# Attention backward for two blocks: x^T and g^T from transposing DMAs, all transfers on one chained queue, group products 512 + 128 wide

## The chip, the cores and the metric

The kernel runs on one core of one Trainium2 chip. The metric is the device time of one execution, in microseconds (us). Each kernel was run several times, and before every comparison the kernel before was run on the same chip in the same rounds. Executions of one kernel differ by up to 15 us in the worst case, so differences of a few us in the whole are read with their intervals.

A ratio is the mean time of one kernel's runs over that of the kernel before in the same rounds. It is therefore not quite the ratio of the medians that are quoted beside it. The experiments ran in other rounds than the kernel after, on three chips, and the median of the kernel before went from 1711.5 to 1713.9 us between them; where a run is compared with after, the ratios are therefore the better measure.

## The reference

Two independent attention blocks, A and B, of the same shape; the outputs are laid side by side. The kernel returns the output and the gradients of all ten inputs for a given `grad_out`.

```python
B, Sq, D = 8, 96, 640            # x: [8, 96, 640]
H, Sk, Dh = 32, 512, 128         # k_cache, v_cache: [8, 32, 512, 128]
def _A_ref(x, k_cache, v_cache, wq, wo):          # _B_ref is the same
    q = (x @ wq).reshape(B, Sq, H, Dh).transpose(0, 2, 1, 3)
    scores = einsum("bhqd,bhkd->bhqk", q, k_cache) * Dh ** -0.5
    p = softmax(scores)
    o = einsum("bhqk,bhkd->bhqd", p, v_cache)
    return o.transpose(0, 2, 1, 3).reshape(B, Sq, H * Dh) @ wo
out = concatenate([_A_ref(...), _B_ref(...)], axis=-1)      # [8, 96, 1280]
# returned: out and d(x, k, v, wq, wo) of both blocks, for grad_out [8, 96, 1280]
```

All inputs and outputs are bf16.

## The kernel before

The kernel handles block A, then block B. In a block it works through 32 heads, in pairs that share loads and in groups of four that share the products with wo and wq (here "group products", which sum into `out` and `dx`). One head and one batch entry is a "tick": scores, softmax, and the four gradient products for 96 queries and 512 keys. There are 2 x 32 x 8 = 512 ticks. The instructions are placed by a table of ticks (`em.add(tick, slot, fn)`), so loads, transposes and products of different heads are interleaved in one static order for each engine.

The parts that the change and the argument touch:

```python
class Chain:                       # keeps the issue order of the sync queue as written
    def __call__(self, res):
        ins = getattr(res, "ins", res)
        if self.last is not None:
            self.tc.add_manual_dep(ins, self.last.name, ..., reason="issue order")
        self.last = ins
        return res
...
    def setup_ld(which_, c):       # block B: a column chunk of x or g, by GpSimd
        ...
            nc.gpsimd.dma_start(tmp[:], src_flat[:, c * 128:(c + 1) * 128].rearrange("(t p) d -> p t d", p=128))
    def setup_T(which_, c):        # x^T and g^T by TensorE, 6 transposes a chunk, and a copy on VectorE
        ...
            for t0 in range(0, TT, 8):
                ...
                    nc.tensor.transpose(pt[:, i * 128:(i + 1) * 128], tmp[:, t0 + i, :], ident[:])
                nc.vector.tensor_copy(dst[:, c, t0 * 128:(t0 + nt) * 128], pt[:, 0:nt * 128])
...
    def pA(h):                     # the weights of a head, by GpSimd
            nc.gpsimd.dma_start(wo_h, wo[h * 128:(h + 1) * 128, :])
            ...
                    nc.gpsimd.dma_start(wq_p[:], wq_v[:, :, h * 128:(h + HP) * 128])
...
    def p_st(h, b, which):         # stores of dV and dK of a pair, on the chained sync queue
            sp(nc.sync.dma_start(dst.rearrange("h (p c) d -> p h (c d)", c=KC), t_[:]))
...
                st["dK_p"] = wk.tile([128, HP, KC * 128], BF16, name="dK_sb", bufs=3)   # dV_sb: bufs=3 too
...
    gsplits = [(0, 256), (256, 256), (512, 128)]      # built by a loop in the kernel
    def gU(g, which, t, gi):       # group products, 256 + 256 + 128 wide
            ...
            else:                  # last group: each piece is stored by GpSimd at once
                ob = wk.tile([128, w], BF16, name="ob", bufs=4)
                nc.vector.tensor_tensor(ob[:], o_ps[:], acc[:, t, c0:c0 + w], op=ALU.add)
                nc.gpsimd.dma_start(dst_flat[t * 128:(t + 1) * 128, c0:c0 + w], ob[:])
```

The loads of K, V (natural and transposed) and the stores of dK and dV are on the sync queue already; the transposed forms KT and VT come from transposing DMAs.

Of the kernel before, what the change touches and what calls it, by code (L numbers as in the profile page):

```python
# [8 lines left out]
ALU = mybir.AluOpType  # L9
AX = mybir.AxisListType  # L10
F32 = mybir.dt.float32
BF16 = mybir.dt.bfloat16
# [3 lines left out]
class Emitter:  # L16
# [28 lines left out]
HP = 2  # L45
HK = [
    dict(pA=-10, pB=-7, pC0=[-6, -4], pC1=[-5, -3], pD1=-2, pD0=0, qA0=21, qA1=25, qB=[28, 25], qD=[(26, 0, 2), (27, 2, 5)]),
    dict(pA=-4, pB=-2, pC0=[-1, 3], pC1=[1, 2], pD1=3, pD0=6, qA0=29, qA1=33, qB=[36, 33], qD=[(34, 0, 2), (35, 2, 5)]),
# [23 lines left out]
def build_block(tc, em, tick0, blk, x, kc, vc, wq, wo, g_all, out_all, dx, dk, dv, dwq, dwo, ident, ones, pools, HG=4, first=True, groups=None):  # L72
# [47 lines left out]
    stp = pools["stp"]  # L120
    sp = pools["sp"]

    def setup_ld(which_, c):
        def f():
            src_flat = x_flat if which_ == 0 else g_flat
            tmp = stp.tile([128, TT, 128], BF16, name="ld_tmp")
            with nc.allow_non_contiguous_dma(reason="setup column chunk"):
                nc.gpsimd.dma_start(tmp[:], src_flat[:, c * 128:(c + 1) * 128].rearrange("(t p) d -> p t d", p=128))
            S[("tmp", which_, c)] = tmp
        return f  # L130

    def setup_T(which_, c):
        def f():
            key = "xT" if which_ == 0 else "gT"
            if c == 0:
                S[key] = const.tile([128, DC, T], BF16, name=key, bufs=1)
            dst = S[key]
            if first:
                tmp = S["x_nat" if which_ == 0 else "g_nat"][:, :, c * 128:(c + 1) * 128]
            else:  # L140
                tmp = S.pop(("tmp", which_, c))
            for t0 in range(0, TT, 8):
                nt = min(8, TT - t0)
                pt = bank([128, 8 * 128], BF16, "tp_ps")
                for i in range(nt):
                    nc.tensor.transpose(pt[:, i * 128:(i + 1) * 128], tmp[:, t0 + i, :], ident[:])
                nc.vector.tensor_copy(dst[:, c, t0 * 128:(t0 + nt) * 128], pt[:, 0:nt * 128])
        return f

    def setup_nat(which_):  # L150
        def f():
# [3 lines left out]
            (nc.sync if first else nc.gpsimd).dma_start(t_[:], src_flat.rearrange("(t p) d -> p t d", p=128))  # L155
# [8 lines left out]
    for c in range(DC):  # L164
        if not first:
            em.add(tick0 - 12 + c - 2, SL_LOAD, setup_ld(0, c))
            em.add(tick0 - 11 + c - 2, SL_LOAD, setup_ld(1, c))
        em.add(tick0 - 12 + c, SL_SETUP, setup_T(0, c))
        em.add(tick0 - 11 + c, SL_SETUP, setup_T(1, c))
    em.add(tick0 + (-15 if first else 21), SL_LOAD, setup_nat(1))  # L170
    em.add(tick0 + (-16 if first else 20), SL_LOAD, setup_nat(0))
# [10 lines left out]
    def pA(h):  # L182
        def f():
# [4 lines left out]
            nc.gpsimd.dma_start(wo_h, wo[h * 128:(h + 1) * 128, :])  # L188
            j = h % HP
            if j == 0:  # L190
                wq_p = hd.tile([128, DC, HP * 128], BF16, name="wq_p", bufs=2)
                with nc.allow_non_contiguous_dma(reason="per-pair wq slice"):
                    nc.gpsimd.dma_start(wq_p[:], wq_v[:, :, h * 128:(h + HP) * 128])
# [266 lines left out]
    def qB(h, di):  # L460
        def f():
            st = HS[(blk, h)]
            Onat = st["Onat"]
            if "dwo_sb" not in st:
                st["dwo_sb"] = hd.tile([128, D], BF16, name="dwo_sb")
                st["dwo_n"] = 0
# [6 lines left out]
            st["dwo_n"] += 1  # L473
            if st["dwo_n"] == len(dsplits):
                nc.gpsimd.dma_start(dwo[h * 128:(h + 1) * 128, :], dwo_sb[:])  # L475
        return f

    def qD(h, c_lo, c_hi):
        def f():
# [4 lines left out]
            if "dwq_sb" not in pr:  # L484
                pr["dwq_sb"] = hd.tile([128, DC, HP * 128], BF16, name="dwq_sb", bufs=1)
                pr["dwq_n"] = 0
# [9 lines left out]
            pr["dwq_n"] += ncn  # L496
            if pr["dwq_n"] == DC * HP:
                with nc.allow_non_contiguous_dma(reason="per-pair dwq slice"):
                    nc.gpsimd.dma_start(dwq_v[:, :, (h - j) * 128:(h - j + HP) * 128], dwq_sb[:])  # L499
# [8 lines left out]
    gsplits = []  # L508
    c0_ = 0
    while c0_ < D:  # L510
        w_ = 256 if D - c0_ >= 256 else 128
        gsplits.append((c0_, w_))
        c0_ += w_

    def gU(g, which, t, gi):
        def f():
            acc = S.get("out_acc" if which == 0 else "dx_acc")
            dst_flat = out_flat if which == 0 else dx_flat
            (c0, w) = gsplits[gi]
# [199 lines left out]
```

## Time and profile before

The kernel before takes 1711.03 us (three runs, 1708.27 to 1713.91); the profiled run spans 1706.8 us.

The page's first and third part (busy time and share of the span for each engine; the DMA queues with packets, MB and the time of their packets as a share of 16 engines' span):

```profile
PE 1633.9 (96%) x22648; PEld 1359.3 (80%) x22648; DVE 1388.8 (81%) x3597; ACT 1345.0 (79%) x3529; POOL 713.3 (42%) x1306
...
q1 hardware_dynamic: 304672, 404.75, 91.3%
q0 software_dynamic: 15648, 49.83, 8.2%
```

TensorE is busy 96% of the span, but the DMA queues' shares also sum to about 1. The view by windows (the stretch, its length, the busy time and instruction count of each engine, the granted TensorE clock, the DMA share and GB/s):

```profile
core 0: us, PE busy (x) PEld busy (x) DVE busy (x) ACT busy (x) POOL busy (x), PEclk, DMA share, GB/s
...
25.00:109.00 84.00, 76.61 (x1066) 61.38 (x1065) 69.66 (x175) 76.93 (x201) 35.14 (x65) 1.00 1.01 267
109.00:211.00 102.00, 101.03 (x1411) 84.03 (x1409) 79.11 (x193) 92.21 (x253) 41.48 (x76) 1.00 1.05 280
...
778.00:954.00 176.00, 158.38 (x2144) 131.19 (x2142) 134.14 (x345) 125.25 (x324) 89.57 (x158) 0.96 0.98 264
954.00:1055.00 101.00, 100.22 (x1399) 83.31 (x1397) 78.30 (x191) 91.38 (x252) 41.13 (x76) 1.00 1.03 278
...
1664.00:1707.00 43.00, 30.29 (x388) 25.80 (x385) 23.40 (x62) 9.09 (x24) 25.20 (x46) 0.90 0.29 106
```

In the stretch from 109 to 211 us TensorE is busy 101.03 of 102 us. In the first 84 us after the start it is busy 76.61 only. At the seam of the blocks (778 to 954) TensorE is idle 17.6 us and the clock falls to 0.96. At the end the DMAs move 106 GB/s and the clock falls to 0.90.

The waits at the seam (780 to 930 us; waiting engine, line and tile <- releaser: us in total, times, longest), and the longest of VectorE's as a row of its timeline (start, duration, engine, line, operation, count, [idle before <- releaser]):

```profile
DVE ob L536 <- DMA out_dram<-ob: 6.1, 4, 2.7
PE tp_ps L146 <- DMA ld_tmp<-in_B_x_dram: 5.8, 4, 3.0
```

```profile
908.77 0.43 DVE L536 TENSOR_TENSOR ob<-o_ps,dx_acc 128x256 bf16<-128x256 f32 x1 [2.71 <-DMA out_dram<-ob]
```

VectorE waits for the narrow output stores of block A, which stand behind the 960 KB loads of x_nat and g_nat on GpSimd's queue; TensorE waits for the chunks that it is to transpose.

### The profile page before, as it was taken

How to read it: one execution, taken by the hardware profiler on the slowest of the kernel's cores; microseconds unless marked ns; L12 is line 12 of the kernel's file. 1: busy time of each engine (PE TensorE's matmuls, PEld its weight loads, DVE VectorE, ACT ScalarE, POOL GpSimd, SP SyncE). 2: the span in 40 equal slices, each digit the busy share in tenths (PEclk: the TensorE clock that was granted, in tenths of full speed). 3: DMA queues.
4: the chain of work that ended last, by engine and by line, in shares of the span. 5: the costliest groups of instructions: out<-in, count | busy, mean ns of one | idle time of the engine just before them, and what ended most of it. 6: DMA issues, size and time to landing. Idle time of an engine off the chain costs nothing. (4 is left out here: it accounts for less than half of the span.)

```text
span 1706.8 us, 59407 instructions
## 1 busy us (share of the span) xinstructions
PE 1633.9 (96%) x22648; PEld 1359.3 (80%) x22648; DVE 1388.8 (81%) x3597; ACT 1345.0 (79%) x3529; POOL 713.3 (42%) x1306
## 2 busy tenths in 40 slices
PE   6999999999999999998998999999999999999997
PEld 4788888887888888786876888878888788887876
DVE  4887888888888888887876878888888888888885
ACT  4988977878788787875876989787787877878782
POOL 3443343444334443344464444343443343443345
PEclk9999999999999999999998999999999999999999
DMA  9999999999999999999999999999999999999992
GB/s 257 278 277 279 281 271 274 286 285 273 280 266 267 284 267 275 266 276 264 251 284 273 274 269 291 266 265 284 275 272 268 270 271 289 269 273 276 255 258 106
DMA packets 320608, 458.38 MB, mean 269 GB/s; under 512 B 37217, under 2 KB 300897, under 8 KB 312129
## 3 DMA queue, kind: packets, MB, share of 16 engines
q1 hardware_dynamic: 304672, 404.75, 91.3%
q0 software_dynamic: 15648, 49.83, 8.2%
q8 instruction: 177, 2.90, 0.7%
q14 instruction: 111, 0.90, 0.1%
HBM read 161.09 MB, written 159.12 MB: 188 GB/s over the span
## 5 line engine op out<-in xcount | busy, mean ns | idle before, releaser
L313 ACT ACTIVATE E_sb<-S_ps,negm 96x512 bf16<-96x512 f32 x512 | 349.7, 683 | 218.7 <-DVE negm L303 208.9
L332 POOL TENSOR_SCALAR P_sb<-E_sb,rinv 96x512 bf16<-96x512 bf16 x512 | 354.3, 692 | 318.8 <-DVE rinv L323 313.4
L386 POOL TENSOR_TENSOR prod<-OT_h,dOT_h 128x96 bf16<-128x96 bf16 x512 | 188.1, 367 | 532.6 <-DVE OT_h L358 527.9
L400 DVE SCALAR_TENSOR_TENSOR dS_sb<-dP_ps,dl_ps,P_sb 96x512 bf16<-96x512 f32 x512 | 382.2, 746 | 30.0 <-PE dl_ps L398 17.7
L303 DVE TENSOR_REDUCE negm<-S_ps 96x1 f32<-96x512 f32 x512 | 347.9, 680 | 43.8 <-PE S_ps L301 42.8
L443 ACT ACTIVATE dK_sb<-dK_ps 128x512 bf16<-128x512 f32 x512 | 302.6, 591 | 74.1 <-PE dK_ps L438 70.4
L377 ACT ACTIVATE dV_sb<-dV_ps 128x512 bf16<-128x512 f32 x512 | 308.1, 602 | 0.3 <-PE dV_ps L372 0.2
L361 ACT ACTIVATE PT_sb<-optp_ps 128x384 bf16<-128x384 bf16 x512 | 252.3, 493 | 0.7 <-PE optp_ps L355 0.5
L372 PE MATMUL dV_ps<-dOnat_h,P_sb 96*128 96x128 bf16 x2048 | 198.7, 219 | 0.0
L438 PE MATMUL dK_ps<-Qnat_h,dS_sb 96*128 96x128 bf16 x2048 | 198.4, 219 | 0.0
L422 PE MATMUL dq_dst_ps<-ident,dS_sb 96*128 96x96 bf16 x2048 | 172.8, 206 | 25.9 <-DVE dS_sb L400 23.9
L396 PE MATMUL dP_ps<-VT_p,dOT_h 128*96 128x512 bf16 x512 | 195.7, 382 | 0.0
L301 PE MATMUL S_ps<-KT_p,QT_h 128*96 128x512 bf16 x512 | 194.5, 380 | 0.4
L424 DVE COPY dST_sb<-dq_dst_ps 128x384 bf16<-128x384 bf16 x512 | 177.6, 347 | 12.9 <-PE dq_dst_ps L422 12.1
L355 PE MATMUL optp_ps<-ident,P_sb 96*128 96x96 bf16 x2048 | 172.2, 206 | 2.4 <-POOL P_sb L332 1.7
L348 PE MATMUL optp_ps<-PT_sb,V_sb 128*128 128x96 bf16 x2048 | 172.3, 206 | 0.9 <-ACT PT_sb L361 0.8
L415 PE MATMUL dq_dst_ps<-dST_sb,K_sb 128*128 128x96 bf16 x2048 | 170.9, 206 | 1.7 <-DVE dST_sb L424 1.5
L525 PE MATMUL o_ps<-wo_r,OT_h 128*128 128x256 bf16 (+1 forms) x1152 | 150.5, 254 | 1.4
L415 PEld LDWEIGHTS <-K_sb 128*128 128x128 bf16 x2048 | 134.1, 98 | 21.8 <-issue 2.6
L525 PE MATMUL o_ps<-wqT_h,dQT_h 128*128 128x256 bf16 (+1 forms) x1152 | 150.3, 255 | 0.5 <-DVE ob L536 0.5
L358 DVE CAST OT_h<-optp_ps 128x96 bf16<-128x96 f32 x512 | 126.7, 247 | 19.3 <-PE optp_ps L355 16.0
L422 PEld LDWEIGHTS <-dS_sb 96*128 96x128 bf16 x2048 | 114.8, 98 | 33.7 <-DVE dS_sb L400 32.2
(77 smaller groups left out, 3369.7 us busy)
## 6 DMA issues: line engine op xcount, KB each, us to landing
out_dram<-dV_sb SPq DMA_DIRECT2D x256, 256.0 KB, 4.5
out_dram<-dK_sb SPq DMA_DIRECT2D x256, 256.0 KB, 4.9
V_sb<-in_A_v_cache_dram SPq DMA_DIRECT2D x128, 256.0 KB, 4.8
K_sb<-in_A_k_cache_dram SPq DMA_DIRECT2D x128, 256.0 KB, 4.8
V_sb<-in_B_v_cache_dram SPq DMA_DIRECT2D x128, 256.0 KB, 4.8
K_sb<-in_B_k_cache_dram SPq DMA_DIRECT2D x128, 256.0 KB, 4.8
out_dram<-dwo_sb POOLq DMA_DIRECT2D x64, 160.0 KB, 4.9
out_dram<-dwq_sb POOLq DMA_DIRECT2D x32, 320.0 KB, 6.0
```

Of the source, the lines that this page charges most:

```text
L303: nc.vector.tensor_reduce(negm[:], S_ps[:], axis=AX.X, op=ALU.max, negate=True)
L313: nc.scalar.activation(E_sb[:].rearrange("q (a f) -> q a f", f=F4), st["S_ps"][:].rearrange("q (f a) -> q a f", f=F4), ACT.Exp, bias=st["n ...
L332: nc.gpsimd.tensor_scalar(P_sb[:], st["E_sb"][:], st["rinv"][:], 0.0, op0=ALU.mult, op1=ALU.add)
L361: nc.scalar.activation(PT_sb[:], PT_ps, ACT.Identity, scale=1.0)
L372: nc.tensor.matmul(dV_ps[:, c * 128:(c + 1) * 128], P_sb[:, c * 128:(c + 1) * 128], hs["dOnat_h"][:, b * 128:(b + 1) * 128], start=True, s ...
L377: nc.scalar.activation(dV_p[:, j], dV_ps[:], ACT.Identity, scale=1.0)
L400: nc.vector.scalar_tensor_tensor(dS_sb[:].rearrange("q (a f) -> q a f", f=F4), dP_ps[:].rearrange("q (f a) -> q a f", f=F4), dl_ps[:, 0:1] ...
L415: nc.tensor.matmul(dQT_ps, st["K_sb"][:, c, :], st["dST_sb"][:, c * Sq:(c + 1) * Sq], start=(c == 0), stop=(c == KC - 1))
L422: nc.tensor.transpose(dST_ps[:, c * Sq:(c + 1) * Sq], dS_sb[:, c * 128:(c + 1) * 128], ident[0:Sq, 0:Sq])
L438: nc.tensor.matmul(dK_ps[:, c * 128:(c + 1) * 128], dS_sb[:, c * 128:(c + 1) * 128], hs["Qnat_h"][:, b * 128:(b + 1) * 128], start=True, s ...
L443: nc.scalar.activation(dK_p[:, j], dK_ps[:], ACT.Identity, scale=1.0)
L525: nc.tensor.matmul(o_ps[:], src[:, t * 128:(t + 1) * 128], rhs, start=(hh == 0), stop=(hh == groups[g] - 1))
```

## The change

The intent is to take work off TensorE and VectorE (the transposes of x and g and their copies), to take all DMA issue off GpSimd, and to have fewer and wider group products with one store of 640 columns for three narrow ones. The core of the diff:

```diff
     def setup_T(which_, c):
-            dst = S[key]
-            ...                      # x_nat/g_nat (block A) or ld_tmp (block B), 6 transposes, copy
-                    nc.tensor.transpose(pt[:, i * 128:(i + 1) * 128], tmp[:, t0 + i, :], ident[:])
-                nc.vector.tensor_copy(dst[:, c, t0 * 128:(t0 + nt) * 128], pt[:, 0:nt * 128])
+            src_flat = x_flat if which_ == 0 else g_flat
+            sp(nc.sync.dma_start_transpose(S[key][:, c, :], src_flat[:, c * 128:(c + 1) * 128]))
     def setup_nat(which_):
-            (nc.sync if first else nc.gpsimd).dma_start(t_[:], src_flat.rearrange("(t p) d -> p t d", p=128))
+            sp(nc.sync.dma_start(t_[:], src_flat.rearrange("(t p) d -> p t d", p=128)))
-        em.add(tick0 - 12 + c, SL_SETUP, setup_T(0, c))          # and the others
-    em.add(tick0 + (-15 if first else 21), SL_LOAD, setup_nat(1))
+        em.add(tick0 + (-10 if first else -11 + c // 3), SL_LOAD + 0.5, setup_T(0, c))
+    em.add(tick0 + (8 if first else 22), SL_LOAD + 0.5, setup_nat(1))
     def pA(h):
-            nc.gpsimd.dma_start(wo_h, wo[h * 128:(h + 1) * 128, :])
+            sp(nc.sync.dma_start(wo_h, wo[h * 128:(h + 1) * 128, :]))    # wq_p likewise
+    def qB_st(h): ...               # the dwo and dwq stores: sync queue, two ticks after their product
+            sp(nc.sync.dma_start(dwo[h * 128:(h + 1) * 128, :], HS[(blk, h)]["dwo_sb"][:]))
-    gsplits ...                     # 256 + 256 + 128
+    def gU(g, which, t, di):        # 512 + 128, as the other products are split
+    def gU_st(g, which, t):         # one store of 640 columns, two ticks later
+            sp(nc.sync.dma_start(dst_flat[t * 128:(t + 1) * 128, :], G[(g, which, t)][:]))
```

In block A the natural loads x_nat and g_nat move from the very start to tick 8 and 9: they are no longer needed for the transposes. Not shown in this cut: the wo load of each pair's second head is issued three ticks earlier (`pA` from -4 to -7).

## The prediction

> **What bounds it now.** TensorE. The page has PE busy 1633.9 of 1706.8 us (96%), DVE 81%, ACT 79%, POOL 42%. In the steady part (timeline of PE) one stall before the dS transposes returns every 102.55 us (489.77, 592.33, 694.88): one group of four heads. Pitches there: 217 ns for 512 columns, 108 for 256, 57 for 128, as in the Trainium skill ("TensorE: Matmul & The Clock Gate", Back-to-back issue gap: N/2.4 + 2.5 ns). Charging every matmul so, I estimate 98.6 us of array time per group (4% to gain). DMA looks full (share about 1.0), but PE waits for no load there, and the sync queue waits some 900 us for PE and ACT to free buffers: it is not the limit.
>
> Sixteen groups make 1641 us. The other 66 us are what the change can reach:
> - start: PE first works at 6.0, then waits 5.8 us for g; first score matmul at 24.7 us;
> - seam of the blocks: 694.88 to 1128.71 us is 433.8 us, four groups and 23.6 us. PE waits 7.8 us for ld_tmp around 790-808 us; around 906-923 us DVE waits for out-stores (2.7+1.1+1.6 us) behind the 960 KB g_nat load (12.1 us to land), PE then idles 5.2+1.5+1.2 us, and the clock is 0.83 and 0.91 in those two 20 us stretches;
> - tail: PE ends near 1696 us, then 11 us of narrow out-stores issued by POOL at 0.5 us each.
>
> **What the change does.**
> - Removes 120 transposes on PE (60 in the seam, 56 ns each: 3.4 us), 20 DVE copies (11 us, off the path), and the ld_tmp waits. Adds 20 transposing DMAs of 192 KB; one of 256 KB holds the sync queue 1.1 us and lands after 5.4.
> - Group products: 768 fewer matmuls, same columns: about 2 us of PE. DVE per 640 columns: 0.415+0.415+0.278 becomes (estimate) 0.69+0.28: 27 us less, not limiting.
> - POOL loses about 180 us of DMA issue. It rarely holds PE (waits on P_sb 5 us, prod 11).
> - The sync queue gains some 4.5 us per pair of heads (51 us), beside about 34 busy: it fits. Stores are queued two ticks (6.4 us) after their producer, like dV. The Trainium skill ("DMA: Bandwidth & Descriptors", Issuing engines are not separate DMA queues) says all issuers share the 16 engines: no bandwidth gained. New risk: bursts of 1.92 MB (x^T with g^T; x_nat with g_nat) stand before K and V loads; at about 280 GB/s 7 us of delay, against an estimated 8 us of slack.
>
> **Sum (estimates).** Start -4, seam -14, tail -6, steady part -3: 27 us. Predicted 1684 us (-1.6%), 8 in 10 between 1666 and 1704. Faster by over 2%: 0.29; within 2%: 0.66; slower: 0.05.
>
> **To check.** No wait of PE on x^T or g^T, first score matmul near 19 us; seam surplus near 10 us instead of 23.6, clock about 1.0, no DVE wait on out-stores; span ends 5-6 us after the last matmul; group period still 102-103 us; POOL near 31%; 21760 matmuls.
>
> **What would make it wrong.** The instruction order around the wider products may shift: the 1.41 us stall of each group could vanish or double, plus or minus 16 us. The bursts may starve K/V loads at the seam or near 45 us, where x_nat and g_nat now load. A store waiting in the single queue may delay loads behind it in every pair. Transposing at a 1280-byte pitch may be slow.

## More of the kernel before

Note the three buffers of `dK_sb` and `dV_sb`: a buffer holds one batch entry of a pair of heads (256 KB), and can be written again only when its store has landed.

ScalarE's waits for stores of dK, over the whole run (there is no line for dV):

```profile
ACT dK_sb L443 <- DMA out_dram<-dK_sb: 0.2, 1, 0.2
```

This is the line to remember: before the change, the three dK buffers are practically always free in time, though sometimes only just. From the trace, the median time from the landing of a store to the next write of its buffer is 8.6 us, but it falls below 1 us five times, between reductions 20 and 70 (a reduction marks a tick, see below).

## The result

The kernel after takes 1700.93 us (median of four runs, 1700.71 to 1701.99), against 1711.47 us for the kernel before (four runs, 1708.27 to 1713.91): ratio 0.9941, 95% interval 0.9923 to 0.9958. "Within 2%" was the likeliest in the prediction and the time lies in its range, but the gain is some 10 us, not 27.

The same lines of the page as above:

```profile
PE 1622.0 (95%) x21526; PEld 1277.7 (75%) x21760; DVE 1363.6 (80%) x3409; ACT 1344.4 (79%) x3505; POOL 535.1 (31%) x1030
...
q1 hardware_dynamic: 386112, 456.54, 102.0%
```

GpSimd is at 31%, as predicted; the software queue q0 is gone. The view by windows, with the columns as above; the borders are the same ticks as before, so each row does the same heads:

```profile
0.00:24.00 24.00, 13.78 (x66) 7.09 (x68) 2.75 (x6) 4.88 (x7) 0.70 (x6) 1.00 0.85 186
24.00:116.00 92.00, 77.03 (x1051) 61.27 (x1057) 69.66 (x174) 76.85 (x201) 32.64 (x62) 1.00 1.07 276
116.00:223.00 107.00, 101.82 (x1357) 80.63 (x1370) 78.94 (x194) 91.62 (x242) 33.69 (x65) 0.98 1.04 274
...
788.00:950.00 162.00, 150.43 (x1977) 118.66 (x1995) 126.07 (x317) 123.73 (x323) 49.62 (x96) 0.98 1.04 280
950.00:1057.00 107.00, 101.70 (x1347) 80.22 (x1360) 78.61 (x193) 91.35 (x242) 33.53 (x65) 0.98 1.02 272
...
1665.00:1699.00 34.00, 29.44 (x331) 20.81 (x333) 21.69 (x49) 8.90 (x24) 2.38 (x5) 1.00 0.38 132
```

The seam has fallen from 176 to 162 us and the tail from 43 to 34. But the first group of block A takes 92 us instead of 84 and the second 107 instead of 102, the second of block B 107 instead of 101. TensorE's busy time in these rows is nearly what it was (77.03 and 76.61; 101.82 and 101.03): it waits more.

For exact borders I use the ticks: VectorE's max-reduction of the scores (`negm`) occurs exactly 512 times in each trace, once for each tick. A group of four heads is 32 reductions, and block B begins at reduction 256. So 288 to 320 is the second group of block B, although some of the texts call it the first. The stretches between reductions number a and b, in us, from the profiled runs:

```
reductions   start-0   0-32   32-64  64-240 240-288 288-320 320-496 496-511 511-end   span
before         25.15  83.52  102.03  567.02  175.92  101.74  566.41   42.14   42.89  1706.83
after          24.46  91.74  106.57  565.06  162.67  106.96  566.13   41.15   34.19  1698.93
difference     -0.69  +8.22   +4.54   -1.96  -13.25   +5.22   -0.28   -0.99   -8.70    -7.90
```

Seam and tail gain 22.0 us together, and the steady parts 3.2 (64-240, 320-496 and 496-511). The start gains 0.7 instead of 4. And 18.0 us (8.22 + 4.54 + 5.22) are lost in three stretches for which the prediction's sum has no loss, though its list of risks names late loads and the single queue. The prediction fails on these last two points.

What is new in those stretches? ScalarE's waits for stores, the line that was 0.2 us before:

```profile
ACT dK_sb L421 <- DMA out_dram<-dK_sb: 23.2, 11, 5.1
...
ACT dV_sb L355 <- DMA out_dram<-dV_sb: 3.0, 2, 2.0
```

Three rows of the timeline, ScalarE's at 137 and at 820 us and TensorE's right after the first:

```profile
137.29 0.60 ACT L421 ACTIVATE dK_sb<-dK_ps 128x512 bf16<-128x512 f32 x1 [3.12 <-DMA out_dram<-dK_sb]
```

```profile
820.53 0.60 ACT L421 ACTIVATE dK_sb<-dK_ps 128x512 bf16<-128x512 f32 x1 [5.15 <-DMA out_dram<-dK_sb]
```

```profile
137.94 0.69 PE L182 MATMUL woT_ps<-ident,wo_r 128*128 128x128 bf16 x5 [2.79 <-ACT dK_sb L421]
```

ScalarE cannot move dK out of PSUM (the memory that TensorE writes its sums to) because the store of three batch entries ago has not landed; 2.79 us of it reach TensorE. The data of that store had been complete since the end of this move, at 121.63 us:

```profile
121.05 0.58 ACT L421 ACTIVATE dK_sb<-dK_ps 128x512 bf16<-128x512 f32 x1
```

The sync queue just before the wait (SPq: rows of the queue; start and duration of the issue):

```profile
129.39 1.17 SPq L239 DMA_TRANSPOSE VT_p<-in_A_v_cache_dram  x1
130.62 0.56 SPq L166 DMA_DIRECT2D wo_r<-in_A_wo_dram  x1
131.24 0.42 SPq L171 DMA_DIRECT2D wq_p<-in_A_wq_dram  x1
131.70 0.52 SPq L250 DMA_DIRECT2D K_sb<-in_A_k_cache_dram  x1
132.33 0.65 SPq L259 DMA_DIRECT2D out_dram<-dK_sb  x1
```

The dK store is issued at 132.33 us, behind loads of VT, wo, wq and K that all stand in the one queue now; it lands at about 137.2. So of the 15.6 us from data to landing, 10.7 were the wait for its turn: twelve other transfers were issued in that time, three of which (dwq, wo, wq; 1.4 us of issue) the change had brought into the queue. Over the whole run the median wait for its turn of a dK store is 1.3 us in before and 4.4 in after, and the median time from a landing to the next write of the buffer falls from 8.6 to 5.8 us.

Comparing single ticks over all runs shows how local this is. Against the shortest time of the same tick in any run, after is slow at reduction 13 (+2.3 us), 31 (+1.8), 39 (+4.5), 249 and 250 (+6.5 and +2.5) and 295 (+4.5). Before has no such tick below 240. Reductions 39, 295 and, in other kernels, 71, 103, 135, 167, 263 and so on are all the eighth tick of a group.

The start, TensorE's timeline of after:

```profile
5.74 0.58 PE L212 MATMUL q_ps<-xT,wq_p 128*128 128x512 bf16 x1 [0.67 <-DMA xT<-in_A_x_dram]
...
10.61 0.58 PE L212 MATMUL q_ps<-xT,wq_p 128*128 128x512 bf16 x1 [0.76 <-DMA xT<-in_A_x_dram]
12.11 0.59 PE L212 MATMUL q_ps<-gT,woT_h 128*128 128x512 bf16 x1 [0.91 <-DMA gT<-in_grad_out_dram]
...
16.85 0.59 PE L212 MATMUL q_ps<-gT,woT_h 128*128 128x512 bf16 x1 [0.30 <-DMA gT<-in_grad_out_dram]
...
24.04 0.38 PE L279 MATMUL S_ps<-KT_p,QT_h 128*96 128x512 bf16 x1
```

and the sync queue's:

```profile
1.66 6.51 SPq L128 DMA_TRANSPOSE xT<-in_A_x_dram  x5
8.21 6.57 SPq L128 DMA_TRANSPOSE gT<-in_grad_out_dram  x5
...
15.45 2.39 SPq L239 DMA_TRANSPOSE KT_p<-in_A_k_cache_dram  x2
```

The same in before:

```profile
6.04 0.82 PE L146 MATMUL tp_ps<-ident,x_nat 128*128 128x128 bf16 x6 [6.04 <-DMA x_nat<-in_A_x_dram]
12.66 0.82 PE L146 MATMUL tp_ps<-ident,g_nat 128*128 128x128 bf16 x6 [5.80 <-DMA g_nat<-in_grad_out_dram]
...
24.74 0.38 PE L301 MATMUL S_ps<-KT_p,QT_h 128*96 128x512 bf16 x1
```

Each transposing DMA holds the queue 1.3 us (6.51 us for five), so the ten of x and g are issued by 14.8 us; g^T's last chunk is there at 16.85. TensorE has waited chunk by chunk, and it stays at half its rate: the five products of 256 columns that start at 17.23 us follow each other at 0.213 us, those at 24.26 us at 0.109 (a single product of 512 columns shows 0.58 us here and 0.38 later). In TensorE's order the products with g^T stand before the first scores, which come at 24.04 us, 0.7 earlier than before. That explains the missing start gain. It does not explain the 18 us.

### The profile page after: what moved, and what is told of

The parts are those of the page before. It is cut to its first block, busy times and chain, and to the rows that moved or that the text cites. A ratio compares the mean times of both kernels' runs of the same rounds, so it can differ in the third digit from the quotient of the medians. Undisturbed runs are those within 1.5% of the kernel's fastest.

```text
span 1698.9 us, 57158 instructions
## 1 busy us (share of the span) xinstructions
PE 1622.0 (95%) x21526; PEld 1277.7 (75%) x21760; DVE 1363.6 (80%) x3409; ACT 1344.4 (79%) x3505; POOL 535.1 (31%) x1030
## 3 DMA queue, kind: packets, MB, share of 16 engines
q8 instruction: 170, 2.79, 0.7%
## 5 line engine op out<-in xcount | busy, mean ns | idle before, releaser
L279 PE MATMUL S_ps<-KT_p,QT_h 128*96 128x512 bf16 x512 | 194.4, 380 | 10.7 <-ACT dK_sb L421 8.9
L402 DVE COPY dST_sb<-dq_dst_ps 128x384 bf16<-128x384 bf16 x512 | 177.1, 346 | 14.0 <-PE dq_dst_ps L400 13.9
L497 PE MATMUL o_ps<-wqT_h,dQT_h 128*128 128x128 bf16 (+1 forms) x706 | 143.2, 292 | 3.3
L497 PE MATMUL o_ps<-wo_r,OT_h 128*128 128x128 bf16 (+1 forms) x707 | 142.5, 294 | 3.5 <-issue 0.4
```

The lines of the kernel that those rows point to most:

```text
L497: nc.tensor.matmul(o_ps[:], src[:, t * 128:(t + 1) * 128], rhs, start=(hh == 0), stop=(hh == groups[g] - 1))
```

## The experiments

Fifteen kernels were run. In the texts, B names the theory that bytes are the limit: in the first groups of each block the DMAs move all they can, and what the change moved there costs time, wherever it stands. The rival, in its forms O, Q, F and K, is that something about the one queue makes single transfers late: the number of issues, their order, the stores' place, or too few buffers behind it. All outputs were correct. The stretches come from one profiled run each. It lies more than 3 us from the median for b_gu and e10 (their fastest, 1692.67 and 1686.76 us) and for e8, u_T and e13 (their slowest, 1713.35, 1712.62 and 1696.18 us).

```
run           what it is                                         us (range)                     ratio [95%]
b_T           before + transposing DMAs only                     1711.07 (1710.20 to 1712.96)   0.9999 [0.9972, 1.0026]
b_gu          before + wide products and output stores only      1700.88 (1692.67 to 1702.20)   0.9928 [0.9893, 0.9963]
e5_gu256      after, products 256+256+128 as before              1706.32 (1703.27 to 1709.48)   0.9966 [0.9940, 0.9991]
e2_w_pool     after, weights and their/out stores on GpSimd      1704.32 (1703.19 to 1708.50)   0.9957 [0.9936, 0.9977]
e1_nat_pool   after, x_nat and g_nat on GpSimd                   1709.75 (1709.58 to 1712.32)   0.9988 [0.9970, 1.0005]
u_T           after, transposes by TensorE                       1708.82 (1701.98 to 1712.62)   0.9968 [0.9938, 0.9998]
e8_T1         after, one transposing DMA for five                1709.11 (1708.95 to 1713.35)   0.9974 [0.9944, 1.0003]
e7_split      after, K and V loads in halves                     1778.24 (1776.48 to 1785.21)   1.0398 [1.0363, 1.0432]
e3_dk4        after, 4 dK buffers                                1699.62 (1695.10 to 1703.26)   0.9924 [0.9899, 0.9949]
e6_hybrid     after, block A transposed by TensorE               1698.22 (1688.64 to 1703.71)   0.9910 [0.9860, 0.9960]
e9_w_after    after, weights behind the dK/dV stores             1724.86 (1721.97 to 1726.85)   1.0065 [1.0038, 1.0091]
e10_best      e6 + e9's edit + 4 dK and 4 dV buffers             1690.91 (1686.76 to 1694.56)   0.9869 [0.9846, 0.9893]
e11_st44      after, 4 dK and 4 dV buffers                       1694.53 (1691.54 to 1696.66)   0.9888 [0.9867, 0.9909]
e13_st_pool   after, dK and dV stores on GpSimd                  1690.57 (1685.31 to 1696.18)   0.9856 [0.9828, 0.9884]
e12_hyb44     e6 + 4 dK and 4 dV buffers                         1683.84 (1682.83 to 1687.82)   0.9831 [0.9811, 0.9852]
```

The same stretches as above for each, in us, from the profiled runs, with ScalarE's waits for dK and dV stores in the last column:

```
reductions   start-0   0-32   32-64  64-240 240-288 288-320 320-496 511-end | waits for stores
before         25.15  83.52  102.03  567.02  175.92  101.74  566.41   42.89 |  0.2
after          24.46  91.74  106.57  565.06  162.67  106.96  566.13   34.19 | 26.2
b_T            32.57  91.26  102.08  566.78  162.72  102.83  567.09   43.75 | 14.3
b_gu           25.90  86.49  101.97  565.25  164.52  104.48  565.47   35.65 |  3.7
e5_gu256       25.27  91.51  102.90  567.58  168.31  106.26  566.38   33.54 | 27.7
e2_w_pool      30.55  90.79  103.12  565.34  163.45  107.03  565.44   36.07 | 20.8
e1_nat_pool    34.38  85.14  103.34  568.11  166.98  106.86  567.38   34.54 | 25.7
u_T            22.03  87.28  110.49  566.80  175.02  108.03  565.24   34.77 | 24.0
e8_T1          21.61  91.38  107.76  573.18  160.78  109.10  572.39   34.21 | 36.8
e7_split       24.02  97.24  109.46  590.04  176.04  108.04  594.51   34.20 | 78.4
e3_dk4         24.77  89.85  103.30  567.18  166.99  103.85  565.04   34.19 | 13.9
e6_hybrid      21.39  85.11  108.80  570.22  168.98  103.27  565.41   34.33 | 23.5
e9_w_after     25.15  94.89  108.93  574.09  173.85  106.07  565.73   34.18 | 35.1
e10_best       21.19  83.46  103.74  565.33  163.12  107.46  565.15   34.35 |  0
e11_st44       24.64  89.29  103.15  564.92  165.44  103.84  564.93   34.21 |  0
e13_st_pool    24.58  89.00  102.56  568.20  165.96  102.29  566.04   34.27 |  0
e12_hyb44      21.89  83.44  103.46  565.04  165.19  101.97  565.28   34.35 |  0
```

### The two halves alone

b_gu is the kernel before with the new `gU` and `gU_st` (512 + 128, one store of 640 columns, still issued by GpSimd). b_T is the kernel before with the new `setup_T` and `setup_nat` alone:

```diff
-                nc.gpsimd.dma_start(dst_flat[...c0:c0 + w], ob[:])          # b_gu
+            nc.gpsimd.dma_start(dst_flat[t * 128:(t + 1) * 128, :], G[(g, which, t)][:])
-                    nc.tensor.transpose(...)                                # b_T
+            sp(nc.sync.dma_start_transpose(S[key][:, c, :], src_flat[:, c * 128:(c + 1) * 128]))
```

> Before with only the group products 512+128 wide and the output tiles stored 640 columns wide (24 stores of 160 KB instead of 72 of 64 and 32 KB), still from GpSimd. If width makes the tail's gain (42.9 to 34.2 us after reduction 511): tail 35 to 37 us; steady stretches 64 to 240 and 320 to 496 down by 0 to 3 us each; seam 240 to 320 down by 2 to 6 us, since DVE no longer waits for narrow output buffers behind g_nat (5 us there); whole about 1697 to 1702. If the tail's gain came from the sync queue, tail stays at 41 to 43 and the whole above 1704.

> Before with only the transposing DMAs for x^T and g^T and after's places for x_nat and g_nat (sync queue); weights, their gradients and the outputs stay on GpSimd, group products 256+256+128. If the transposes and the moved loads alone make both the gain at the seam and the loss in the first groups: reduction 32 at 114 to 118 us, reductions 240 to 320 take 268 to 272 us (before 277.7), tail as before 42 to 44 us, whole 1706 to 1712. If the seam's gain needs the single queue, 240 to 320 stays above 275 and the whole is over 1715.

The wide products and their stores alone have the whole net gain: 1700.88 us, as after. Their trace, of the fastest run, gains 7.2 us in the tail and 11.4 at the seam (no more waits of VectorE for narrow output buffers). The transposing DMAs alone gain 13.2 us at the seam and lose 7.4 at the start, which the forecast did not have, and 7.7 in the first group: nothing on the sum. So the change is a good half and a half that gives back what it wins; its third part, the weights on the sync queue, is taken out by e2 below. The two gains at the seam do not add (11.4 and 13.2 alone, 13.3 in after): in after, reductions 249 and 250 lose 9.0 us there, with ScalarE waiting for dV and dK stores.

### Width of the products, and the weights' queue

e5_gu256 puts the split of before into after. e2_w_pool puts the loads of wo and wq and the stores of dwo, dwq and out back on GpSimd:

```diff
+    gsplits = [(0, 256), (256, 256), (512, 128)]                            # e5
-            sp(nc.sync.dma_start(wo_h, wo[h * 128:(h + 1) * 128, :]))       # e2, and the four others
+            nc.gpsimd.dma_start(wo_h, wo[h * 128:(h + 1) * 128, :])
```

> After with the group products 256+256+128 wide again (one store of 640 columns per token tile kept). Theory W (width): 768 more matmuls at 2.3 ns and 27 us more DVE; the steady stall of 1.41 us before the dS transposes comes back, group period 102.1 to 102.5 us, whole +4 to +8 us. Rival: the steady gain came from GpSimd's relief, the width is worth 0.1 us a group: whole within 2 us of after. Reductions 0 to 64 stay near 198 us in both, since no group product decides there.

> After with the loads of wo and wq and the stores of dwo, dwq, out and dx back on GpSimd (unchained), transposes and x_nat, g_nat still on sync. Order on PE, DVE and ACT unchanged. Theory O (occupancy of the sync queue): about 7 us of issue less in each group on sync; the first groups are where the queue never rests (84.7 of 91.7 us issuing), so 0 to 64 falls by 3 to 6 us; steady group period stays 102.1 us. Rival P (GpSimd relief): the steady gain of 0.4 us a group came from freeing GpSimd, so the period goes back to about 102.5 and the whole gets 5 us worse; tail 3 to 5 us longer in either case. If neither, whole within 3 us of after.

In undisturbed groups the period of four heads is 102.55 us with narrow products (before, e5) and 102.13 with wide ones (after, b_gu, e2): 0.42 us a group, some 6.7 us if all sixteen had it. e5 is 5.4 us slower than after by the medians, which fits, although the intervals of the ratios overlap. e2 keeps the 102.13, so freeing GpSimd is worth nothing in the steady part; it costs 6.1 us at the start, where after's weights come first in the sync queue, and 1.9 in the tail, and its whole is 3.4 us slower than after by the medians, with overlapping intervals. With the weights off the chained queue the stretch 32-64 falls to 103.12 us, but 288-320 stays at 107.03 and 20.8 us of waits for stores remain: the weights alone do not make the stores late.

### Block A's natural loads

> After with only the x_nat and g_nat loads (1.92 MB per block) issued by GpSimd; for block A GpSimd issues them at the very start, for block B where they were. Order on PE, DVE and ACT unchanged. Theory Q (queue): these two loads stand before K, V and stores in the single queue and make them late; off the queue reductions 288 to 320 fall from 107 to about 102 us and 0 to 64 to about 188, start longer by 2 to 5 us because 1.92 MB more go in the first 15 us: whole about 1690. Rival B (bytes): block B moves the same bytes at the same time, so 288 to 320 stays at 106 to 108; block A only shifts the loss to the start: whole 1698 to 1702.

```diff
-            sp(nc.sync.dma_start(t_[:], src_flat.rearrange("(t p) d -> p t d", p=128)))
+            nc.gpsimd.dma_start(t_[:], src_flat.rearrange("(t p) d -> p t d", p=128))
```

Off the chained queue, the 1.92 MB of x_nat and g_nat are no longer held at tick 8 of block A; GpSimd issues them early, beside the transposing DMAs. The first group falls to 85.14 us, but the start rises to 34.38: the sum of both is 119.5 us instead of 116.2. The bytes cost time wherever they stand in the first 120 us. The whole, 1709.75 us, is slower than both theories had it. The stretch 288-320 in block B is unchanged (106.86), so it is not these loads that hurt there.

### The number and the form of the DMAs

e7_split loads K and V in two DMAs of 128 KB for one of 256 KB: 512 more DMAs, the same bytes. e8_T1 makes one transposing DMA for all of x, and one for g, where after has five each:

```diff
+            [sp(nc.sync.dma_start(t_[:, j]..., src[j]...)) for j in range(HP)]                        # e7
+            c or sp(nc.sync.dma_start_transpose(S[key][:], src_flat))                                # e8
```

> After with each natural-layout load of K and V (256 KB, 0.57 us of the sync queue) issued as two DMAs of 128 KB, one for each head: same bytes, 512 more DMAs, an estimated 1.0 us more of the queue for each pair of ticks. Order on PE the same, two neighbouring swaps on DVE and ACT. Theory O (the queue's issuing is the limit of the first group, 84.7 of 91.7 us issuing): reductions 0 to 32 get 10 to 16 us longer. Theory B (bytes at the DMA engines are the limit[...]): 0 to 32 within 3 us of after's 91.7, the transposing DMAs just hold the queue for less. Whole: over 1712 under O, under 1706 under B.

> After, with one transposing DMA for the whole of x and one for g in each block in place of five each: 10 DMAs become 2 per tensor pair, the bytes and the arithmetic order stay. Theory I (each transposing DMA costs queue time, 1.28 us for 192 KB in after, and this serial issue is what starves the start): the issue time per KB falls, g^T is there by about 10 us instead of 16.85, the first score matmul is at 18 to 20 us instead of 24.0, the whole is 3 to 6 us below after. Theory R (the transposition itself runs at about 150 GB/s, or slower in one large piece): g^T lands as late as before, 16 to 18 us, PE even waits for the whole of x^T before its first product instead of for one chunk, the stretch before the first max-reduction is 25 to 28 us and the whole equals after or is 1 to 4 us above.

e7 is 77 us slower than after. Its waits for stores:

```profile
ACT dK_sb L421 <- DMA out_dram<-dK_sb: 77.8, 29, 5.5
```

The loss sits at the same spot again, the eighth tick of the groups, 4 to 5 us each in most of them, now in the steady part too. So the same bytes in more DMAs bring the stalls of after everywhere: the queue is close to a limit in the steady part also, only just on its right side. The stretch 0-32 grows by 5.5 us, which lies between the two forecasts; the whole speaks for theory O.

e8's start shows what the transposing DMAs can give. The sync queue:

```profile
1.66 4.86 SPq L128 DMA_TRANSPOSE xT<-in_A_x_dram  x1
6.57 4.32 SPq L128 DMA_TRANSPOSE gT<-in_grad_out_dram  x1
```

and TensorE:

```profile
13.06 2.29 PE L212 MATMUL q_ps<-gT,woT_h 128*128 128x512 bf16 x5 [1.49 <-DMA gT<-in_grad_out_dram]
...
21.20 0.38 PE L279 MATMUL S_ps<-KT_p,QT_h 128*96 128x512 bf16 x1
```

The issue of x^T falls from 6.51 to 4.86 us, g^T is there at 13.06 instead of 16.85, and the first scores come at 21.20: 2.8 us earlier than in after. Both theories are half right: the queue time of x^T falls by a quarter (of both by 30%), but the transposition itself still takes the larger part. The whole is yet 8 us slower than after by the medians (the intervals of the ratios just overlap), because three groups of the steady part now stall (reductions 135, 167 and 359; +2.4, +4.5 and +5.3 us against after), which no account of the start explains. The edit touches only the setup of the two blocks, so a small change there can bring stalls hundreds of us away. How it does so was not followed up.

### Undoing the transposing DMAs inside after

> After with its transposing DMAs undone alone: x^T and g^T by TensorE as in before, with all loads and stores still in the one chained queue and the products still 512+128 wide. What it tells is the worth of the transposing DMAs inside after. If they are worth nothing on the sum, as the change's transposing part alone showed on before (1711.1 against 1711.5): reduction 32 at 106 to 110 us instead of 116.2, the seam stretch 240 to 288 at 164 to 168 us instead of 162.7, the whole 1690 to 1699 us, at or a little below after. If they are worth the 12 us that the seam gained, 1705 to 1712 us.

u_T takes the setup of before (natural loads first, `ld_tmp`, transposes on TensorE) with everything on the chained queue. It is 7.9 us slower than after by the medians, the second of the two outcomes, though its runs spread over 10.6 us and the intervals of the ratios overlap. The seam is back at 175.02 us, and the first group is 4.5 us shorter. But the second group takes 110.49 us, the longest of all runs, with a 7.2 us stall at reduction 39, and the waits for stores are 24.0 us. So the stalls do not need the transposing DMAs of x and g. They do not need the weights in the queue either: b_T, without them, has 14.3 us of these waits. What the runs with long waits share is more in the chained queue than in before, not one kind of transfer.

### Buffers for dK, order of the weights, block A on TensorE

```diff
-                st["dK_p"] = wk.tile([128, HP, KC * 128], BF16, name="dK_sb", bufs=3)    # e3
+                st["dK_p"] = wk.tile([128, HP, KC * 128], BF16, name="dK_sb", bufs=4)
-            em.add(c0t + hk["pA"], SL_LOAD, pA(h))                                       # e9
+            em.add(c0t + hk["pA"], SL_LOAD + 0.4, pA(h))
+            if first:                                                                    # e6: block A
+                tmp = S["x_nat" if which_ == 0 else "g_nat"][:, :, c * 128:(c + 1) * 128]
+                ...                      # six transposes on TensorE and the copy, as in before
-    em.add(tick0 + (8 if first else 22), SL_LOAD + 0.5, setup_nat(1))
+    em.add(tick0 + (-15 if first else 22), SL_LOAD + 0.5, setup_nat(1))
```

> After with four instead of three buffers for the pairs of dK on their way out; instruction order on every engine is the same as in after. Theory S (slack): the 18 us lost in the first groups of each block (max-reductions 0 to 64: 198.3 us against 185.6 in before; 288 to 320: 107.0 against 101.8) are ScalarE waiting to evacuate dK until an old dK store has landed (11 waits, 23 us), the store being late in the one sync queue; a fourth buffer gives it 2 more ticks: those waits fall below 3 us, reductions 0 to 64 take about 188 us, 288 to 320 about 102, the whole about 1685 us. Rival B (bytes): the first group is limited by what the DMA engines move, a buffer moves no byte: 0 to 64 stays above 195 us, the wait reappears at another tile (dV, or PE on KT or VT), the whole 1697 to 1702.

> After, with the loads of wo and wq put behind the dK and dV stores of the same tick in the chained queue, nothing else; same bytes, same compute order. Theory Q (the stores of dK land late because they stand behind a burst of loads in the single queue, and the late landing is what holds ScalarE, then PE): the ScalarE waits of 3.1 us at 137.3 us and 3.2 us at 971.7 us for a dK store go or halve, reductions 32 to 64 take about 103 us instead of 106.6, the same in the second block, the whole is 4 to 8 us below after. Theory B (in the first groups of each block the bytes exceed what the DMAs move in that time): the waits move to other tiles, the two stretches change by less than 1.5 us each and the whole stays within 2.5 us of after.

> After, except that block A gets x^T and g^T by TensorE from x_nat and g_nat loaded first, as in before; block B keeps its transposing DMAs. 1.92 MB of DMA fewer at the start. Theory B (bytes): up to max-reduction 32 the kernel runs at the pace of its DMA (before 108.7 us, after 116.2; the difference 7.5 us is 1.92 MB at about 270 GB/s): reduction 32 comes at 107 to 110 us, reductions 32 to 64 take 102 to 104 us, later stretches as in after (64 to 240: 565; seam 163 and 107; tail 34): whole about 1688 us, below both kernels. Rival: the loss is the order of work or the single queue (weights and stores on it), then reduction 32 stays at 114 or later and the whole above 1695.

With a fourth dK buffer alone the waits for dK stores go, but waits for dV stores take their place (13.9 us, 12 times), and the whole changes by 1.3 us, within the spread. Read alone, this looks like proof that the waits only move; it was half an experiment, as e11 shows.

e9 was a miss for both theories: 24 us slower than after. The waits for stores rise to 35.1 us, and a new wait appears:

```profile
PE woT_ps L182 <- DMA wo_r<-in_B_wo_dram: 6.8, 2, 5.2
```

The weights are loaded only few ticks ahead; moved back in the queue, they are late themselves. The order of the queue was not free to change. Since the stores, now ahead of the weights, wait longer and not less, this speaks against the weights just before them as what makes them late.

e6 brings block A's transposes back to TensorE and keeps the transposing DMAs for block B. Reduction 32 comes at 106.50 us instead of 116.20 (3.1 us of it in the start), and the first group takes 85.11 us instead of 91.74, so most of the first group's loss is the bytes that the change brings into it. By the view of windows, after moves 276 GB/s for 92 us there, 25.4 MB; before 267 for 84 us, 22.4 MB. Two of these three MB are x_nat and g_nat; where the third comes from was not followed up. But the stall at reduction 39 grows to 6.4 us, others come at 103 and 263, and its runs range over 15 us, so the forecast of about 1688 us for the whole and of 102 to 104 for 32-64 (108.80) failed.

### The two causes apart, and the version that beats both

> A version meant to beat both: after, with block 1's x^T and g^T made by TensorE from the natural loads as in before (saves 1.9 MB in the first group), the second block's by transposing DMAs as in after, the wo and wq loads behind the dK and dV stores of their tick, and four buffers instead of three for the dK and dV stores (rowsum from three to two buffers to fit). Theory Q+B (bytes in the first group and order in the queue together make the loss): reduction 32 near 106 us, reductions 32 to 64 near 103 us, the second block's first group near 103 us, the whole 1682 to 1690 us, 11 to 18 us below after, with less spread than the 1688.6 to 1703.7 of the version without the last two edits. If instead the dK waits only move (B alone): 1694 to 1699 us.

e10 had three edits at once: e6's, e9's and four buffers for both dK and dV. It beats both kernels, at 1690.91 us, just above its forecast, with no wait for a store left, but TensorE waits 7.2 us for wo of block B, and 288-320 takes 107.46 us instead of the forecast 103. Since e9 alone was harmful, the last three runs took the edits apart.

```diff
-                rowsum = wk.tile([Sq, 1], F32, name="rowsum", bufs=3)         # e11, e12: makes room
+                rowsum = wk.tile([Sq, 1], F32, name="rowsum", bufs=2)
-  ... name="dV_sb", bufs=3)   ... name="dK_sb", bufs=3)
+  ... name="dV_sb", bufs=4)   ... name="dK_sb", bufs=4)
-            sp(nc.sync.dma_start(dst.rearrange("h (p c) d -> p h (c d)", c=KC), t_[:]))    # e13 alone
+            nc.gpsimd.dma_start(dst.rearrange("h (p c) d -> p h (c d)", c=KC), t_[:])
```

> After, with four buffers instead of three for both the dK and the dV stores (rowsum from three to two to fit), nothing else; same instruction order on every engine, same bytes. Theory K (the single-tick stalls are waits for a store buffer): no wait of ScalarE on a dK or dV store is left, the extra 4 to 6 us at reductions 39, 249 and 295 go, reductions 32 to 64 take 103 to 104 us, 288 to 320 some 103, the whole 1690 to 1695 us (after: 1700.9). Theory B (throughput): the stalls come back as waits for KT, wo or g_nat at nearly the same ticks, the whole 1697 to 1702 us.

> The version with block 1 transposed on TensorE, four dK and four dV buffers, but with the weights in after's place in the queue (ahead of the stores). Against the three-edit version (1690.9 us) it lacks only the weights' move. In that version PE waited 7.2 us for wo in the second block's first groups. Theory K: these waits go and no others come, 288 to 320 takes about 103 us instead of 107.5, the whole is 1682 to 1688 us. Theory B: another load is late in its place, the whole stays at 1689 to 1693 us.

> After, with the dK and dV stores issued by GpSimd instead of the chained sync queue, three buffers as in after; same bytes. Theory F (the stores are late because of their place behind loads in one queue): ScalarE's waits for stores (23.2 us for dK, 3.0 for dV) go to nearly nothing, the sync queue loses some 14% of its issues, reduction 64 comes at 212 to 216 us instead of 222.8, the whole 1688 to 1694 us. Theory B (throughput of the DMAs): stores and loads now share it in parallel, the stalls move to loads or stay, the whole 1697 to 1703 us. A third outcome: GpSimd holds each store 1 us or more while it waits its turn behind GpSimd's own work, and the stores land later than before; then it is slower than after.

e11 has the same instructions in the same order on every engine as after; it differs by buffers alone. From a landing to the next write of the buffer there are now at least 2.3 us, where after has 0.08 at its waits. No wait of ScalarE for a store is left, and the same move of dK that waited until 137.29 us in after now follows without a gap:

```profile
131.57 0.32 ACT L153 ACTIVATE out_acc<-o_ps 128x128 f32<-128x128 f32 x1
131.77 0.61 ACT L421 ACTIVATE dK_sb<-dK_ps 128x512 bf16<-128x512 f32 x1
```

The stretches 0-32, 32-64 and 288-320 fall by 2.45, 3.42 and 3.12 us, the whole by 6.4 by the medians and by about 9 by the ratios (0.9888 against 0.9941, intervals apart). The first group still takes 89.29 us; TensorE now waits for loads there (the lines are of the whole run; the longest wait of the first, 2.9 us, lies in the first group):

```profile
PE S_ps L279 <- DMA KT_p<-in_A_k_cache_dram: 3.5, 2, 2.9
...
PE dq_dst_ps L393 <- DMA K_sb<-in_A_k_cache_dram: 1.9, 3, 1.0
```

Some of the gain is given back at the seam (+2.8 us), where TensorE now waits 5.8 us for g_nat: that much of theory B stands.

e13 keeps three buffers and takes the stores out of the chained queue. The waits for stores go as well, although a dK store now takes longer from issue to landing (median 5.4 us instead of 4.6), and the whole falls by 10.4 us by the medians (intervals of the ratios apart). So it was not the speed of a store but the moment of its issue: in the chained queue it waited for what was ahead of it. The trace shows this: the median dK store is issued 0.3 us after its data are complete (4.4 in after), at most 1.6 us (17.3). The edit also takes 512 of 1776 issues out of the chained queue, so it does not tell the order in that queue from its load. Two remedies, deeper buffers and another queue, remove the same stalls; one would do.

e12 has the buffers and block A on TensorE, with the weights in after's place. It is the best version, 1683.84 us, ratio 0.9831 (0.9811 to 0.9852), 17 us below after. Its windows for the first two groups (columns as above):

```profile
22.00:105.00 83.00, 75.66 (x1052) 60.43 (x1051) 68.83 (x173) 76.00 (x200) 32.47 (x62) 1.00 1.00 263
105.00:209.00 104.00, 101.48 (x1372) 79.72 (x1371) 79.02 (x195) 91.57 (x242) 33.84 (x65) 1.00 1.06 290
```

The first group moves 263 GB/s for 83 us, 21.8 MB, and takes what it took before. In the second it moves 290 GB/s, more than before (280) or after (274) in theirs: the DMAs could do more than after asked of them there, so throughput was not the cause of after's loss in the second group. In the first, e13 moves 291 GB/s and still takes 89.00 us: what is left there without waits for stores, and goes in e12, is the bytes.

## Why the prediction was wrong

**Right: the tail, and the waits that go at the seam.** Predicted -6 us for the tail, measured -8.7. Predicted -14 for the seam; VectorE's waits for output stores and TensorE's for `ld_tmp` are gone, and 240-288 gains 13.3. But the prediction drew the seam from 694.88 to 1128.71 us, which is reductions 214 to 342, and between these the gain is only 7.7 us (433.83 to 426.11): it holds the loss of 5.2 in 288-320, and a new wait for a store (5.15 us at 820) already costs part of the gain before it. b_gu gets most of seam and tail alone, b_T gets the seam by its own way. Of the other marks set, GpSimd's 31% and the 21760 matmuls were hit.

**Right: the steady part.** Predicted -3 us; the stretches 64-240, 320-496 and 496-511 gain 3.2 together. It is the width that does it, not the freed GpSimd (the periods of e5 against those of e2).

**Wrong: the start.** Predicted -4 us, with no wait on x^T or g^T and the first scores "near 19 us". Measured -0.7, at 24.04. The failing step was that a transposing DMA of 192 KB would cost little: it holds the queue 1.3 us, ten stand before the first K, TensorE waits for them one by one and runs at half its rate meanwhile, and its order asks for g^T before the scores. The prediction named "transposing at a 1280-byte pitch may be slow" as a risk; e8 shows that the count of DMAs is a quarter to a third of that queue time.

**Wrong: "DMA looks full, but ... it is not the limit", and "it fits".** This is the step that cost most, 18.0 us in three stretches. It was drawn from TensorE waiting for no load in the steady part. Two things were missed.

1. In block A's first group TensorE has less work for each tick: it is busy 76.61 us over 32 ticks in before, against 101.03 in the second. The DMAs already move 267 GB/s there, so there is little room for more, although no engine waits for a load yet. The change moved x_nat and g_nat (two loads of 960 KB) into this stretch; at 276 GB/s that is about 7 us, an estimate. 8.2 were measured. Two pairs of runs part them: keeping these bytes out is worth 6.6 us with three buffers (e6 against after) and 5.9 with four (e12 against e11), the fourth buffers 2.5 and 1.7. The prediction did say that bursts might starve the loads, and weighed them against "8 us of slack" of the loads. In after TensorE indeed waits for no K or V load; only when the waits for stores are gone (e11) does it wait for KT there, 2.9 us once. The dK buffers had less than 1 us to spare at reductions 20, 22, 36 and 38 already in before, and they were not in the sum.

2. "Room in the queue" was counted in issue time, not in how late a store may land, and the count itself was low: "about 34 busy" of 51 us for a pair of heads. In the trace of before the queue issues for 43.6 us per pair in the stretch 64-240 (45.8 in after), because a transposing DMA of K or V, taken at its shortest 1.1 us, holds it for 1.5 us in the median. A dK buffer comes round after three batch entries of a pair. With more in the same queue ahead of it, the dK store lands 1 to 5 us too late at certain ticks, and ScalarE, then TensorE, stands still. The prediction's last risk, "a store waiting in the single queue may delay loads behind it", had the direction reversed: loads delayed the store. e11 (buffers alone) and e13 (queue alone) both remove these waits; e7 (more DMAs) multiplies them. Which of the added transfers does it is not settled: taking out the weights (e2), the natural loads (e1) or the transposing DMAs (u_T) leaves 20.8 to 25.7 us of the 26.2.

The accounts add up. Of the 18.0 us, e11 recovers 9.0 by buffers alone (2.45 + 3.42 + 3.12), and e12 all but 1.6: its three stretches are 83.44, 103.46 and 101.97 us against 83.52, 102.03 and 101.74 in before. Single profiled runs stand behind these figures, so a us here or there is not settled. What decides that a given kernel stalls in one group of the steady part and not in the next (e8, e6, e9) stays open: the runs show where, at the eighth tick of a group, and that deeper buffers end it, not why that group.

**On the Trainium skill in the prediction.** It cites "DMA: Bandwidth & Descriptors", section "Issuing engines are not separate DMA queues": all issuers share the 16 engines, so no bandwidth is gained. The trace agrees on bandwidth (269 GB/s before, 271 after). The same section adds that starting DMAs on several engines saves only the initiator's time, "which is usually small relative to the DMA itself". Here it is not small: between 300 and 400 us the sync queue of after spends 88.5 of 100 us on issues (86.4 already in before), and moving the stores to another engine's queue (e13) saved 10.4 us by the medians. From the first sentence I concluded that merging the queues was harmless, and that was the error.

It also cites "TensorE: Matmul & The Clock Gate", section "Back-to-back issue gap", for the pitches of 217, 108 and 57 ns. Those hold in the traces, and they were not the problem. The same page's "What's actually happening" (Part 1) tells of an array at half its clock after idle time; the start agrees, with 0.213 us from one product of 256 columns to the next at 17 us, against 0.109 at 24 us, and it was left out of the prediction's sum for the start.

## What to carry to other kernels

Before putting more transfers into a queue, look for the buffers that come free only when one of its stores lands, and ask how late that store may be; the queue's average room says nothing about it, and one buffer more for each kind of store, all kinds at once, may be the whole remedy. Read the DMA limit stage by stage: a stage with little compute for each byte may have no room for more transfers even if no engine waits for one yet, and bytes moved into it can then cost nearly their full time, as here. When a large change moves the time little, run its parts alone: here one half had the whole gain, and the other half's gain became visible only after its new wait was removed.

## What the Trainium skill lacked or had wrong

- "DMA: Bandwidth & Descriptors", "Issuing engines are not separate DMA queues" and the rule on spreading DMAs in "Rules for kernel authors": they name the saved issue time as the only effect of several issuers. The runs show another: what stands in one ordered queue lands late for what stands ahead of it. The stores of dK and dV on a second queue took ScalarE's 26.2 us of waits for stores to none, and 10.4 us (by the medians) off the whole, although the median store took longer to land (5.4 us for 4.6).
- The same page, "Rules for kernel authors": transfers under 64 KB are said to pay mostly overhead. What splitting larger ones costs in a queue that is nearly full is not said. Here, 128 KB for 256 KB, 512 more DMAs for the same bytes, cost 77 us, 0.15 us each with the stalls that they brought.
- The same page, "Latency and other measured facts": it gives 261 GB/s for a transposing DMA with a non-contiguous middle dimension and about 350 to 400 for the contiguous case. Neither was reached for x (1280-byte rows): 983,040 bytes in 6.51 us of queue time are 151 GB/s in five DMAs, in 4.86 us 202 GB/s in one.
- "TensorE: Matmul & The Clock Gate", "Back-to-back issue gap": the sustained 81 ns for 128 columns and 131 ns for 512 do not hold here. In after, 18 products of 128 columns, each with its own weights, took 1.17 us, which leaves about 56 ns each with 0.22 us for the last one; 512 columns kept their 217 ns pitch. The page's simpler formula fits.
- No page says that the profile's granted clock can read 1.00 while products run at half rate: in the first 24 us of after it does, with 0.213 us from one 256-column product to the next at 17 us, against 0.109 at 24 us.
